# Moving the first attention unit's key tiles a partition in two parts, and letting the gates share a table load

## The chip, the core and the metric

The kernel runs on one core of a Trainium2 chip. The metric is the device time of one execution in microseconds. Five engines work side by side, each through its own instructions in order: TensorE (PE, with its weight loads as PEld), VectorE (DVE), ScalarE (ACT), GpSimd (POOL) and SyncE (SP, which here only issues DMAs). ACT and POOL issue DMAs too, between their other instructions.

## What is computed

A gated sum of two branches over 2048 tokens of 512 channels, in float32:

```python
g = sigmoid((x * gate_w).sum(-1))
a = attention(x) @ wo      # 32 heads of 16; each token sees 8 keys, at distances 0, 2, ... 14
b = (gelu(x @ w_gate) * (x @ w_up)) @ w_down      # 1792 hidden channels
out = g * a + (1 - g) * b
```

The attention takes `logits = q . k * 0.25` for the 8 keys, with the keys before the first token masked, a softmax over the 8, and the weighted sum of the values.

## The kernel before

All matrix products run on PE. Each float32 operand is split into a high part (rounded to the fp32r format by ACT) and a low part (the rest, a subtraction on DVE, or on POOL's queue as an accumulating DMA), and each product is three matmuls. Tokens are dealt by parity (`par`): even tokens first, then odd, since keys at even distances have the same parity. Within a parity, partition `p` holds 8 consecutive tokens as slots `j`, so `NP` is 8.

The program for parity 0 is: `start()`, which projects queries and keys for all 8 slots by a Strassen-like scheme with four banks at a time; then `ffn(0)`, 14 hidden blocks `f` of 128 channels, in whose first two blocks the values are projected (`values(jj)`), with the down projection of earlier blocks between the products of later ones. For parity 1 the projections are the plain ones and `ffn(1)` follows. The out projection comes last.

The attention itself runs on DVE beside all that. It is a Python generator, `attention()`, over 8 units of 128 channels, four for each parity: `load_kq` (keys and queries of the unit into the one buffer `kq`), `scores` (four times a product `prod` of line 298 and a sum over 16 channels on line 301, then the mask), `softmax` (max, subtraction on line 314, Exp on ACT on line 316, sum, reciprocal, times the gate `g`) and `mix` (the weighted values). The function `pull` draws on the generator wherever the products of PE leave time by an estimate, and `paced` ties the long operations to the matmul recorded last, so that DVE cannot run ahead of it. The tile framework then schedules all recorded instructions into one fixed order for each engine, by its own estimate of their times.

The first unit is special. Its keys and queries are not read back from DRAM: `take_first` copies them from PSUM straight into `kq` (`put(0)` to `put(3)` early in `start()`, `put(4)` to `put(7)` at its end; the copies stand in the trace as `kq<-p` and `kq<-acc`). Each partition also needs the 7 key slots before its own 8. These are its neighbour's slots, and `load_kq(0, 0)` moves them a partition down by two DMAs on SP's queue (line 276; 112 and 15 partitions of 7 slots of 512 bytes), after POOL has zeroed the first partition's.

The gates, `1 / (1 + exp(-z))` of the column `z` that `take` collects with the values, are computed in `gates(par)` as soon as the last values of a parity are taken (lines 239 to 243): Exp on ACT, three small operations on DVE. ACT's functions come in table sets. Exp and Gelu are in different sets, so an Exp among the Gelus of `gate_up` costs a table load in front of it and another one in front of the next Gelu.

Other lines that the prediction speaks of: 189 (projections on PE), 211 (copies of the values out of PSUM), 436 (sums of the next blocks' weights, `combine`), 454, 455 and 459 (their operands, `g<-raw`: low part by ACT and POOL's DMA, high part), 497 (gate and up products on PE), 502 (`copy`, a PSUM bank into `s`), 507 (`add`, a bank and `s` into `c`), 511, 513 and 514 (`hidden`), 537 (down projection), 571 (a bank copied into another), 586 and 602 (the two Gelus).

Of the kernel before, what the change touches and what calls it, by code (L numbers as in the profile page):

```python
# [16 lines left out]
P = 128  # L17
# [3 lines left out]
NP = NT // 2  # L21
# [16 lines left out]
BT = 4  # L38
# [9 lines left out]
def tile_gated_mix(ctx: ExitStack, tc: tile.TileContext, xt, wqkv, wff, wo, out):  # L48
    nc = tc.nc
# [17 lines left out]
    def bank(tag):  # L67
        return psum.tile([P, 512], F32, name=tag, bufs=BUFS.get(tag, 1))
# [114 lines left out]
    def qkv_mm(ps, par, jj, cb, kcs, c0=0, cn=512):  # L183
        t = slice((jj % BT) * P, (jj % BT + 1) * P)
        for kc in kcs:
            xh, xl = X[par, jj // BT, kc]
            wh, wl = WC[cb, kc]
            for n, (a, w) in enumerate(((xh, wh), (xl, wh), (xh, wl))):
                LAST[:] = [nc.tensor.matmul(ps[:, :cn], a[:, t], w[:, c0:c0 + cn], start=(kc == 0 and n == 0),  # L189
                                            stop=(kc == KC - 1 and n == 2))]  # L190

    KQ = []

    def take_first(ps, jj, copy):

        if not KQ:
            KQ.append(pool.tile([P, 3 * NP - 1, UC], F32, name="kq"))
        st = tl(next(stages))[:, :CU].rearrange("p (a d) -> p a d", a=2)
        two = ps.rearrange("p (a c d) -> p c a d", a=2, c=2)
        copy(KQ[0][:, NP - 1 + jj::NP], two[:, 0])  # L200
        copy(st, two[:, 1])
        for a, t in enumerate((KS[0, 0][1, W:], QS[0, 0][1])):
            nc.sync.dma_start(t.rearrange("(p j) d -> j p d", j=NP)[jj], st[:, a])
# [4 lines left out]
    def take(ps, par, jj, hh, vals, tag=None):  # L208
        st = tl(tag or next(stages))[:, :512]
        n = CU if vals else 512  # L210
        nc.scalar.activation(st[:, :n], ps[:, :n], AF.Copy)
        two = st.rearrange("p (a c d) -> p a c d", a=2, c=2)
        dst = VS[par, hh] if vals else KS[par, hh]
        queue = nc.sync if (vals if par else not vals) or hh and not vals else nc.scalar
        queue.dma_start(rows(dst[:, W:], jj), two[:, 0])  # L215
        if not vals:
            queue.dma_start(rows(QS[par, hh], jj), two[:, 1])
        elif not hh:
            nc.scalar.activation(z[:, par, jj:jj + 1], ps[:, CU:CU + 1], AF.Copy)

    def project(par, cb, bg=iter(())):
        for jj in range(NP):
            if cb == 1:
                for hh in range(2):

                    ps = bank(f"acc{(2 * jj + hh) % BT}")
                    qkv_mm(ps, par, jj, 1, range(KC), (CU, 0)[hh], (WQ, CU)[hh])
                    take(ps, par, jj, hh, True)
            else:
                ps = bank(next(names))  # L230
                qkv_mm(ps, par, jj, 0, range(KC))
                take(ps, par, jj, 0, False)
            next(bg, None)
            pull((2.7, 2.2)[par])
        done.add((par, cb))
        if cb == 1:
            gates(par)

    def gates(par):
        nc.scalar.activation(en, z[:, par], AF.Exp, scale=-1.0)  # L240
        nc.vector.tensor_scalar_add(en, en, 1.0)
        nc.vector.reciprocal(g[:, par], en)
        nc.vector.tensor_scalar(gc[:, par], g[:, par], -1.0, 1.0, op0=OP.mult, op1=OP.add)

    def values(jj):
        for hh in range(2):
            ps = bank(f"acc{(2 * jj + hh) % BT}")
            qkv_mm(ps, 0, jj, 1, range(KC), (CU, 0)[hh], (WQ, CU)[hh])
            take(ps, 0, jj, hh, True, tag=None if jj < 5 else "c")
        pull(2.7)  # L250
        if jj == NP - 1:
            done.add((0, 1))
            gates(0)

    def project_one(par, jj):

# [10 lines left out]
    def load_kq(par, u):  # L267
        hh, c = divmod(u, 2)
        kq = KQ.pop() if KQ else pool.tile([P, 3 * NP - 1, UC], F32, name="kq")
        k, q = kq[:, :2 * NP - 1], kq[:, 2 * NP - 1:]  # L270
        LG[par, u] = k, q
        if not (par or u):

            nc.gpsimd.memset(k[:1, :NP - 1], 0.0)
            for a, b in (1, P - 15), (P - 15, P):
                nc.sync.dma_start(k[a:b, :NP - 1], k[a - 1:b - 1, NP:])
            return
        load_slots(k, KS[par, hh][c])
        nc.sync.dma_start(q, QS[par, hh][c].rearrange("(p j) d -> p j d", j=NP))

    def load_slots(t, src):
        nc.sync.dma_start(t[:, :NP - 1], src[:S // 2].rearrange("(p j) d -> p j d", j=NP)[:, 1:])
        nc.sync.dma_start(t[:, NP - 1:], src[W:].rearrange("(p j) d -> p j d", j=NP))
# [25 lines left out]
    def softmax(par, u):  # L309
        lg = LG[par, u]  # L310
        m = pool.tile([P, UH, NP], F32, name="m")
        nc.vector.tensor_reduce(m, lg, axis=AX.X, op=OP.max)
        yield 0.7
        nc.vector.tensor_tensor(lg, lg, m[:, :, :, None].to_broadcast([P, UH, NP, W]), op=OP.subtract)
        yield 0.7
        nc.scalar.activation(lg, lg, AF.Exp, scale=DH ** -0.5)
        nc.vector.tensor_reduce(m, lg, axis=AX.X, op=OP.add)
        yield 0.7
        nc.vector.reciprocal(m, m)
        nc.vector.tensor_tensor(m, m, g[:, par, None, :].to_broadcast([P, UH, NP]), op=OP.mult)  # L320
        yield 0.4
        nc.vector.tensor_tensor(lg, lg, m[:, :, :, None].to_broadcast([P, UH, NP, W]), op=OP.mult)
        yield 0.7
# [79 lines left out]
    def pull(budget, key=None):  # L403
        credit[0] += budget
        while credit[0] > 0 and (key is None or key not in done):
            with tc.high_priority(offset=-BEHIND):
                c = next(fill, None)
            if c is None:
                credit[0] = 0.0
                return  # L410
            credit[0] -= c
        if key:
            credit[0] = 0.0
# [78 lines left out]
    def product(ps, a, w, start):  # L492
        for kc in range(2):
            ah, al = XOP[a, kc]
            wh, wl = (x[:, kc * P:(kc + 1) * P] for x in w)
            for n, (w_, a_) in enumerate(((wh, ah), (wh, al), (wl, ah))):
                LAST[:] = [nc.tensor.matmul(ps, w_, a_, start=(start and kc == 0 and n == 0),  # L497
                                            stop=(kc == 1 and n == 2), skip_group_check=True)]

    def copy(ps):  # L500
        s = tl("s")
        nc.scalar.activation(s, ps, AF.Copy)  # L502
        return s

    def add(ps, s):
        c = tl("c")[:, :512]
        nc.vector.tensor_tensor(c, ps, s, op=OP.add)  # L507
        return c
# [44 lines left out]
    def gate_up(par, f, pieces, do):  # L553
# [4 lines left out]
        def idle(i, n):  # L558
            for x in do.get(i, ()):
                x()  # L560
            pull(n * PACE[par] * (1.0 if par or f + 1 < FC else 0.8))

        def piece(i):
            for x in pieces[i]:
                x()
# [7 lines left out]
        piece(0)  # L573
        Z_ = bank("p")
        product(Z_, "s1", w["t1"], True)
        p5 = copy(Z_)
        idle(2, 0.3)
# [9 lines left out]
        idle(5, 0.7)  # L587
        product(Z_, "s4", w["b22"], False)
        c12 = add(Z_, u2)
        idle(6, 0.5)  # L590
# [239 lines left out]
    row, act, mms = Row(nc.vector), Row(nc.scalar), Row(nc.tensor)  # L830
# [5 lines left out]
    def start():  # L836
# [98 lines left out]
        def block(ps, a, w, first, kcs=(0, 1)):  # L935
            for t in range(BT):
                for kc in kcs:
                    ah, al = OP_[a, kc]
                    wh, wl = OP_[w, kc]
                    for n, (a_, w_) in enumerate(((ah, wh), (al, wh), (ah, wl))):  # L940
                        mm(ps[t], t, a_, w_, first and kc == 0 and n == 0, kc == 1 and n == 2)
# [10 lines left out]
        def put(jj, ps):  # L952
            take_first(ps, jj, lambda o, i: act.activation(o, i, AF.Copy))
# [29 lines left out]
            lo("t1", k)  # L983
        put(2, V_[2])
        put(3, V_[3])
        Z_ = [bank("p") for _ in range(BT)]
        block(Z_, "s1", "t1", True)
        p5 = [tl("hh")[:, :512] for _ in range(BT)]
# [66 lines left out]
        def sums(f):  # L1055
            r = RAW[f].rearrange("p (a c) -> p a c", c=QW)
            q_ = {n: r[:, i] for i, n in enumerate(QUARTS)}
            sub(r[:, 0:6:5], r[:, 3::4], r[:, 2:4])
            sub(q_["t2"], q_["b22"], q_["t1"])
            sub(q_["t4"], q_["b21"], q_["t2"])  # L1060
# [23 lines left out]
        parts(1)  # L1084
        put(BT + 2, U[2])
        put(BT + 3, U[3])
        sums(1)
        for n, blk, k in (("a11", 0, 0), ("a12", 0, 2), ("a22", 1, 2)):
            for kc in range(2):
# [66 lines left out]
```

## Time and profile before

| | |
|---|---|
| median of 3 runs | 610.23 us (608.02 to 610.64) |
| the profiled execution | 612.35 us, of which its span (first to last instruction) is 610.6 us |
| mean granted TensorE clock | 0.999 |
| PE busy | 598.4 us (98% of the span), 2802 matmuls recorded |
| DVE busy | 526.0 us (86%) |
| ACT busy | 388.7 us (64%) |
| moved by DMA | 131.03 MB, mean 215 GB/s |

A busy PE in this profile is not PE at its peak, since matmuls overlap and their ends are modelled; what the profile shows reliably of PE is where it is not busy and whom it waits for there. A row of a timeline gives start, duration, engine, line, operation, tiles and count, and in brackets the idle time of the engine just before it and what released it. "SPq" and "ACTq" are DMA issues on those queues.

### The profile page before, as it was taken

What the parts mean: (1) busy time and instruction counts of PE and PEld (TensorE: products, weight loads), DVE (VectorE), ACT (ScalarE), POOL (GpSimd) and SP (SyncE); (2) the same over time, 40 slices, a digit from 0 to 9 for tenths busy, and PEclk for the clock granted to TensorE, in tenths of its full rate; (3) what the DMA queues carried; (4) which work ended last, traced back from release to release, by engine and by line L of the source; (5) the groups of instructions that cost most, each with busy time, mean ns of one, the idle gap of its engine ahead of it and who ended that gap; (6) DMA issues with size and microseconds to landing.
All of it is one profiled execution on the core that took longest, in us unless ns stands there. A gap on an engine that the chain in (4) does not pass through costs nothing.

```text
span 610.6 us, 8186 instructions
## 1 busy us (share of the span) xinstructions
PE 598.4 (98%) x2802; PEld 498.0 (82%) x2802; DVE 526.0 (86%) x611; ACT 388.7 (64%) x653; POOL 79.2 (13%) x106
## 2 busy tenths in 40 slices
PE   8999999899999999999999999999999999999996
PEld 6889977778878788888899887888888888888885
DVE  5992798989998888799988997999799979999882
ACT  5844576678666867777374347556865676684722
POOL 0501001111111111102000001111111111101200
PEclk9999999999999999999999999999999999999999
DMA  7288798699898989876689879686878886938714
GB/s 279 70 250 234 205 285 239 159 290 233 229 248 240 266 234 267 219 226 184 204 224 302 275 241 287 163 236 162 248 168 221 210 261 137 279 108 202 91 38 171
DMA packets 84583, 131.03 MB, mean 215 GB/s; under 512 B 7999, under 2 KB 52159, under 8 KB 84542
## 3 DMA queue, kind: packets, MB, share of 16 engines
q1 hardware_dynamic: 63310, 94.27, 47.8%
q0 software_dynamic: 12096, 31.40, 27.0%
q10 hardware_dynamic: 9136, 4.85, 2.6%
q8 instruction: 22, 0.36, 0.2%
q14 instruction: 19, 0.16, 0.1%
HBM read 67.18 MB, written 36.77 MB: 170 GB/s over the span
## 4 chain that ended last, share of the span: by engine, by line
PE 79%; DMA 8%; issue 7%; ACT 2%; DVE 1%; SPq 1%; ACTq 1%; POOL 0%; POOLq 0%; DVEq 0%
PE p L497 35%; PE acc L537 11%; PE p L537 11%; PE acc L189 9%; PE p L763 5%; DMA g<-raw 4%; PE p L828 3%; PE acc L828 2%; PE p L189 2%; PE acc L763 2%; DMA raw<-wff 1%; DMA prod<-wqkv 1%; DMA ws<-g 1%; ACTq L215 1%; DMA vs<-c 1%
## 5 line engine op out<-in xcount | busy, mean ns | idle before, releaser
L497 PE MATMUL p<-S,g 128*128 128x512 f32 x672 | 165.7, 389 | 1.0 <-ACT s L502 1.0
L497 PEld LDWEIGHTS p<-S,g 128*128 128x128 f32 x672 | 125.8, 188 | 27.4 <-ACT s L502 1.4
L497 PE MATMUL p<-A,g 128*128 128x512 f32 x504 | 128.2, 391 | 4.4 <-DMA g<-raw 2.4
L497 PEld LDWEIGHTS p<-A,g 128*128 128x128 f32 x504 | 93.8, 188 | 26.3 <-DMA g<-raw 4.3
L298 DVE TENSOR_TENSOR prod<-kq 128x2048 f32<-128x2048 f32 x32 | 73.1, 2284 | 20.5 <-DMA kq<-kq 14.1
L336 DVE TENSOR_TENSOR prod<-v,lg 128x2048 f32<-128x2048 f32 x32 | 73.0, 2281 | 4.2 <-PE p L497 2.0
L455 POOL DMA_DIRECT2D g<-raw x40 | 34.5, 863 | 316.2 <-ACT g L454 162.3
L301 DVE TENSOR_REDUCE lg<-prod 128x128 f32<-128x2048 f32 x32 | 73.0, 2282 | 0.3
L537 PE MATMUL p<-d,hh 128*128 128x512 f32 x224 | 68.1, 390 | 0.0
L537 PE MATMUL acc<-d,hh 128*128 128x512 f32 x224 | 61.3, 390 | 0.2 <-DMA d<-r 0.2
L502 ACT ACTIVATE s<-p 128x512 f32<-128x512 f32 x56 | 33.3, 595 | 28.7 <-PE p L497 23.6
L537 PEld LDWEIGHTS acc<-d,hh 128*128 128x128 f32 x224 | 41.9, 188 | 9.7 <-DMA d<-r 1.1
L537 PEld LDWEIGHTS p<-d,hh 128*128 128x128 f32 x224 | 42.0, 188 | 8.9 <-ACT hh L513 0.3
L459 ACT ACTIVATE g<-raw 128x1024 fp32r<-128x1024 f32 (+1 forms) x40 | 39.4, 989 | 10.3 <-PE p L497 10.1
L507 DVE TENSOR_TENSOR c<-p,s 128x512 f32<-128x512 f32 x56 | 38.0, 682 | 8.1 <-PE p L497 7.8
L514 DVE TENSOR_TENSOR hl<-c,hh 128x512 fp32r<-128x512 f32 x56 | 38.3, 683 | 7.2 <-ACT hh L513 6.5
L511 DVE TENSOR_TENSOR c<-c 128x512 f32<-128x512 f32 x56 | 38.3, 683 | 6.2 <-ACT c L602 5.9
L537 PE MATMUL p<-d,hl 128*128 128x512 f32 x112 | 42.6, 389 | 0.0
L454 ACT ACTIVATE g<-raw 128x1024 fp32r<-128x1024 f32 (+1 forms) x40 | 39.4, 985 | 4.6 <-DVE raw L436 3.0
L513 ACT ACTIVATE hh<-c 128x512 fp32r<-128x512 f32 x56 | 35.0, 626 | 10.2 <-DVE c L511 10.0
L340 DVE TENSOR_TENSOR prod<-prod 128x1024 f32<-128x1024 f32 x32 | 39.0, 1220 | 0.4
L550 ACT ACTIVATE rt<-p 128x512 f32<-128x512 f32 x48 | 28.2, 593 | 17.4 <-PE p L537 16.9
(194 smaller groups left out, 918.6 us busy)
## 6 DMA issues: line engine op xcount, KB each, us to landing
g<-raw POOLq DMA_DIRECT2D x27, 512.0 KB, 6.8
raw<-wff SPq DMA_DIRECT2D x42, 256.0 KB, 3.7
ws<-g SPq DMA_DIRECT2D x14, 768.0 KB, 6.3
g<-ws SPq DMA_DIRECT2D x14, 768.0 KB, 5.9
r<-wff SPq DMA_DIRECT2D x28, 256.0 KB, 4.1
d<-r POOLq DMA_DIRECT2D x26, 256.0 KB, 6.4
g<-raw POOLq DMA_DIRECT2D x13, 384.0 KB, 7.3
v<-vs SPq DMA_DIRECT2D x8, 512.0 KB, 6.8
```

The lines of the kernel that those rows point to most:

```text
L189: LAST[:] = [nc.tensor.matmul(ps[:, :cn], a[:, t], w[:, c0:c0 + cn], start=(kc == 0 and n == 0), stop=(kc == KC - 1 and n == 2))]
L298: paced(nc.vector.tensor_tensor(prod, spans(k, jj), q[:, jj:jj + 2, None, :].to_broadcast([P, 2, W, UC]), op=OP.mult))
L301: nc.vector.tensor_reduce(two_of(lg, jj), prod.rearrange("p j w (h d) -> p (j w) h d", d=DH), axis=AX.X, op=OP.add)
L336: paced(nc.vector.tensor_tensor(prod.rearrange("p j w (h d) -> p (j w) h d", d=DH), spans(v, jj).rearrange("p j w (h d) -> p j w h d", d=D ...
L340: nc.vector.tensor_tensor(prod[:, :, :4], prod[:, :, :4], prod[:, :, 4:], op=OP.add)
L454: nc.scalar.activation(lo, raw, AF.Copy, scale=-1.0)
L459: ins = nc.scalar.activation(hi, raw, AF.Copy)
L497: LAST[:] = [nc.tensor.matmul(ps, w_, a_, start=(start and kc == 0 and n == 0), stop=(kc == 1 and n == 2), skip_group_check=True)]
L511: nc.vector.tensor_tensor(ge, ge, up, op=OP.mult)
L514: nc.vector.tensor_tensor(hl_, ge, hh_.bitcast(F32), op=OP.subtract)
L537: LAST[:] = [nc.tensor.matmul(pp, a[:, ts], w, start=(i == 0 and n == 0 and gr == 0), stop=(i == 1 and n == 2), skip_group_check=True)]
L763: LAST[:] = [nc.tensor.matmul(pa, a, b, start=(first and n == 0), stop=(last and n == 2), skip_group_check=True)]
```

## The change

`load_kq(0, 0)` no longer issues the two DMAs. `start()` does it through a new helper `shift`: slots 0 to 2 (whose sources `put(1)` to `put(3)` write) by two DMAs on SP's queue right behind `put(3)`, slots 3 to 6 by two DMAs on ACT's queue behind `put(7)`. There `act` is the wrapper that keeps ACT's instructions of `start()` in the order written. The zeroing by POOL moves along with it. And `gates(par)` is no longer called at the end of the values, but from `softmax` of the first unit of each parity, behind its Exp.

```diff
@@ project
         done.add((par, cb))
-        if cb == 1:
-            gates(par)
@@ values
         if jj == NP - 1:
             done.add((0, 1))
-            gates(0)
@@ load_kq
         if not (par or u):
-
-            nc.gpsimd.memset(k[:1, :NP - 1], 0.0)
-            for a, b in (1, P - 15), (P - 15, P):
-                nc.sync.dma_start(k[a:b, :NP - 1], k[a - 1:b - 1, NP:])
             return
@@ softmax
         nc.scalar.activation(lg, lg, AF.Exp, scale=DH ** -0.5)
+        if not u:
+            gates(par)
         nc.vector.tensor_reduce(m, lg, axis=AX.X, op=OP.add)
@@ start
         put(2, V_[2])
         put(3, V_[3])
+        k0 = KQ[0][:, :2 * NP - 1]
+        nc.gpsimd.memset(k0[:1, :NP - 1], 0.0)
+
+        def shift(queue, i, j):
+            for a, b in (1, P - 15), (P - 15, P):
+                queue.dma_start(k0[a:b, i:j], k0[a - 1:b - 1, NP + i:NP + j])
+
+        shift(nc.sync, 0, BT - 1)
...
         put(BT + 2, U[2])
         put(BT + 3, U[3])
+        shift(act, BT - 1, NP - 1)
         sums(1)
```

In the built program the instructions of the engines stand in a partly different order from the first hidden blocks on, since the framework schedules anew. On ACT the two DMA issues stand between the bank copy of line 571 and the first copy of line 502. ACT's table loads fall from 21 to 19.

## The prediction

> **What bounds the kernel now.** I read the page's head first, then the busy time of each engine by stretches of 20 us, then the list of PE's own waits.
>
> ```profile
> span 610.6 us, 8186 instructions
> ```
>
> ```profile
> 40.00:60.00 20.00, 19.99 (x131) 17.95 (x130) 9.76 (x16) 9.24 (x22) 1.79 (x2) 1.00 0.84 231
> ...
> 100.00:120.00 20.00, 17.99 (x78) 14.16 (x77) 20.00 (x22) 13.84 (x23) 2.89 (x4) 1.00 0.59 143
> ...
> 240.00:260.00 20.00, 20.00 (x90) 16.57 (x89) 15.40 (x15) 14.54 (x25) 2.90 (x4) 1.00 0.89 223
> ```
>
> ```profile
> PE p L497 <- DMA g<-raw: 2.4, 3, 1.3
> PE p L497 <- DVE c L507: 2.0, 1, 2.0
> PE p L78 <- DVE zero L72: 1.1, 1, 1.1
> PE p L497 <- ACT s L502: 1.0, 1, 1.0
> ```
>
> The stretches give PE, PEld, DVE, ACT and POOL in that order, then clock, DMA share and GB/s. PE is busy 19.99 of 20 us while the values begin and 20.00 of 20 in the row from 240, so there it sets the pace and nothing that other engines win can show. It falls back in a few places, and the waits name them: 2.4 us for operands that POOL's DMAs complete, 2.0 us for one add on DVE, 1.0 us for one copy on ACT (the 1.1 us are at the start). That is 5.4 us that work on DVE, ACT and the queues could win at most by these rows, 0.9% of the span. The stretch from 100 shows which engine was short: DVE is busy all of its 20.00 us there, PE 17.99.
>
> So the question is whether DVE's and ACT's work around those three places comes earlier or later, and only that.
>
> **Part 1: the shift.** Here are the copy after which ACT is to issue, the shift as it is now, and DVE's first score; then two waits of other engines, and how long the shift's DMAs took to land.
>
> ```profile
> 48.30 0.65 ACT L571 ACTIVATE p<-p 128x512 f32<-128x512 f32 x1
> ...
> 57.49 2.88 SPq L276 DMA_DIRECT2D kq<-kq  x2
> ...
> 64.44 2.29 DVE L298 TENSOR_TENSOR prod<-kq 128x2048 f32<-128x2048 f32 x1 [14.08 <-DMA kq<-kq]
> ```
>
> ```profile
> ACT hh L211 <- DMA qs<-hh: 4.8, 1, 4.8
> ```
>
> ```profile
> SPq L430 <- DVE raw L828: 5.2, 2, 5.0
> ```
>
> ```profile
> DMA to landing us min/median/max: 4.9/5.8/6.7
> ```
>
> The last slots are copied before the bank copy that ends at 48.95. SP gets to the shift at 57.49 only, because other issues stand ahead of it, and DVE sits idle for 14.08 us until 64.44. In the built order of the changed program ACT issues the second part right behind the copy that ends at 48.95. With the first landing at its maximum, 6.7 us, the tiles are there at 48.95 + 6.7 = 55.65; the second DMA, issued half of 2.88 us later and landing in 4.9, comes at 55.3. I take 55.7, which is 8.7 us ahead of now. The bounds: each DMA carries 4 of 7 slots, so a smaller one may land in the 4.9 us (53.9); if the second takes the longest issue and landing together, 48.95 + 2.88 + 6.7 = 58.5.
>
> What ACT pays: two issues, 2.88 us on SP's queue as measured, perhaps less where a queue is quiet. Behind them wait the copy of line 502, the operand casts of line 454 with POOL's DMAs behind these, and the copies of the values. I cost them at nothing, because ACT sits idle for 4.8 us a little later, waiting for the DMA that frees a staging buffer. Without that cover they would cost up to 2.9 us.
>
> The first part goes to SP's queue in front of the loads of line 430, which wait 5.0 us for DVE in that place. It is hidden there, and SP's later issues at 57.49 lose the 2.88 us in front of them. The zeroing on POOL is free at both places.
>
> The moved bytes are the same. But four slots, 127 x 4 x 512 bytes = 0.26 MB, now run between 49 and 56 us, and at the 231 GB/s of the row from 40 this is 1.1 us of all engines' work, in front of the stores for which ACT waits. [...]
>
> **Part 2: the gates.** ACT now, around the gates, with PE's wait behind them:
>
> ```profile
> 79.26 1.28 ACT L240 ACT_TABLE_LOAD   x1 [0.37 <-ACT z L219]
> 80.55 0.21 ACT L240 ACTIVATE en<-z 128x8 f32<-128x8 f32 x1
> ...
> 83.09 1.28 ACT L602 ACT_TABLE_LOAD   x1
> 84.38 0.60 ACT L602 ACTIVATE c<-p 128x512 f32<-128x512 f32 x1
> 84.87 0.59 ACT L502 ACTIVATE s<-p 128x512 f32<-128x512 f32 x1
> ```
>
> ```profile
> 85.52 0.73 PE L497 MATMUL p<-S,g 128*128 128x512 f32 x2 [1.02 <-ACT s L502]
> ```
>
> A load, the small Exp, a load back for Gelu, and only then the copy for which PE stands 1.02 us. In the changed order this pair of loads stays where it is, and the unit's own Exp joins it, directly behind the small one and ahead of everything else. What goes is the unit's own pair of loads, 2 x 1.28 = 2.56 us of ACT some 15 us later, where PE waits for no copy of ACT. So the saving buys nothing, and the Exp moves in front of a copy that PE does wait for.
>
> ```profile
> L298 DVE TENSOR_TENSOR prod<-kq 128x2048 f32<-128x2048 f32 x32 | 73.1, 2284 | 20.5 <-DMA kq<-kq 14.1 <-PE p L497 3.7 <-DMA kq<-qs 1.5
> L301 DVE TENSOR_REDUCE lg<-prod 128x128 f32<-128x2048 f32 x32 | 73.0, 2282 | 0.3
> ...
> L507 DVE TENSOR_TENSOR c<-p,s 128x512 f32<-128x512 f32 x56 | 38.0, 682 | 8.1 <-PE p L497 7.8
> ...
> L436 DVE TENSOR_TENSOR raw<-raw 128x256 f32<-128x256 f32 x24 | 10.0, 418 | 0.1
> ...
> L316 ACT ACTIVATE lg<-lg 128x512 f32<-128x512 f32 x8 | 5.1, 632 | 0.1
> ```
>
> When can that Exp start? It needs the subtraction of line 314. In the changed order of DVE there stand, from the first score to that point, eight long operations and nine short ones: 8 x 2.28 = 18.2 us, and between 9 x 0.42 = 3.8 and 9 x 0.68 = 6.1 for the short ones, 22.0 to 24.3; I take 23.5, nearer to the 0.68 because most of the nine are whole 512-wide adds. From 55.7 that is 79.2. But DVE's first gate operation stands just ahead of the subtraction and waits for the small Exp, which ends at 80.76. So the subtraction ends at about 81.6 (0.16 us, an estimate for the tiny one, and 0.68), and ACT, ready at 80.76, stands 0.84 us and then takes 0.63 us for the Exp. The chain behind it, up to the copy at 84.87, is 1.4 us later, and so is PE: its 1.02 us grow to 2.4. The bounds are 0 (if the copy is not the last thing PE waits for there) and the case of the rival below.
>
> **Part 3: what the lead buys.** The second of the three places, and how the DVE backlog ends:
>
> ```profile
> 107.85 0.68 DVE L507 TENSOR_TENSOR c<-p,s 128x512 f32<-128x512 f32 x1
> ...
> 108.58 0.73 PE L497 MATMUL p<-A,g 128*128 128x512 f32 x2 [2.01 <-DVE c L507]
> ...
> 124.23 0.96 PE L497 MATMUL p<-A,g 128*128 128x512 f32 x3 [1.30 <-DMA g<-raw]
> ...
> 134.91 0.69 DVE L317 TENSOR_REDUCE m<-lg 128x64 f32<-128x512 f32 x1 [3.02 <-ACT lg L316]
> ```
>
> PE stands 2.01 us until the add that begins at 107.85. From 64.44 to 134.91 DVE works off a backlog, and idles for 3.02 us only at its end. An 8.7 us lead reaches into that. In the changed order one long operation more stands ahead of this add (2.28 us, the scheduler spends part of the lead on scores); the wait for the small Exp takes 1.6 us (79.2 to 80.8), and I estimate 1.5 us of new waiting for the second unit's keys: their load waits on the first unit's scores and 1.5 us of idle stand in front of that unit now (the L298 row). Left are 8.7 - 2.28 - 1.6 - 1.5 = 3.3 us: the add begins near 104.5, before PE gets there. This wait goes, 2.0 us.
>
> The waits for POOL's operand DMAs (2.4 us in three places; the one shown ends at 124.23) hang on DVE's sums of line 436 ahead of ACT and POOL. By the same count these are at most a microsecond earlier, and PE arrives 0.6 us earlier, so I leave them as they are. Behind 134.91 DVE is no longer late, and PE's row from 240 has no idle time; whatever is won or lost by then is carried to the end unchanged.
>
> **Sum.** +1.4 (the copy behind the Exp) - 2.0 (the add) + 0 (shift issues) + 0 (operand DMAs) = -0.6 us. The profiled execution took 612.35 us, 1.75 us around its span of 610.6; it would be 611.75. The median of the runs shown is 610.23, 2.1 us below the profiled execution, so I forecast 609.6 us.
>
> **The rivals.**
>
> *The lead cures more.* If DVE's lead reaches ACT and POOL as well, the operand waits vanish with the add's and the copy stays at its 1.02 us: 2.4 + 2.0 = 4.4 us, 610.2 - 4.4 = 605.8 us. For it: DVE's 20.00 of 20 us just where PE falls back, and 14.08 us of idle right before. Against it: the changed order gives the lead to scores first, and one of the operand waits lies beyond 134.91, where DVE is not late any more.
>
> *The Exp stands in ACT's way for longer.* ACT takes its instructions in order, and the unit's Exp stands ahead of the copies. It decides from the point at which DVE is not done with the first unit when the small Exp is: first score later than 80.76 - 23.5 = 57.3. With the upper bound of 58.5 and the short operations at their upper 6.1, the subtraction ends at 58.5 + 24.3 + 0.16 = 83.0 where 81.6 was counted, another 1.4 us; the two issues' 2.88 us uncovered at the same time would not add, since they lie earlier. If in addition the lead is then too small for the add, nothing is taken off, and a third of the operand waits, 0.8 us, comes once more: 610.2 + 1.4 + 1.4 + 0.8 = 613.8 us. For it: a landing of 6.7 us is no exception in these queues, and the changed order was made from estimates of such landings. Against it: 58.5 needs the longest issue and the longest landing at once.
>
> *The crowded DMA engines.* The 1.1 us of part 1 reach PE through ACT's wait for the staging buffer: 609.6 + 1.1 = 610.7 us. Against it: PE's list has no wait for those copies.
>
> *Nothing moves.* If DVE's lead is only turned into idle time and ACT's saving lies off the path, as in the row from 240: 610.2 us.
>
> **How the numbers follow.** About 0.5%, 3.05 us, is what a measurement of this kernel can tell from no change; its three runs lie 2.6 us apart. The forecast has 0.36, crowding 0.12, nothing 0.10: all within 0.5%, 0.58 together. The larger cure, 0.72% below, has 0.22; the longer stand of ACT, 0.59% above, 0.20. The range runs from the one to the other, 605.8 to 613.8, with a tenth of the chance beyond each end.
>
> **What would show it.** In the profile of the changed kernel: DVE's first score at 54 to 58.5 with 4 to 8 us of idle before it; one table load for the small Exp and the unit's Exp near 80, and ACT's idle time before the latter (0.84 us by my count); PE's wait for the copy of line 502 near 86 us at about 2.4; no wait for the add of line 507 near 107; the operand waits at some 2.4 in sum. The forecast is wrong if PE's waits for ACT, DVE and DMA sum to less than 2.4 us or more than 8.5 us, or if PE gets idle time behind 240 us, where it has none now.

## The result, and the profile after

| | before | after |
|---|---|---|
| median (lowest to highest), 20 executions each | 615.67 us (608.02 to 618.12) | 608.28 us (606.52 to 611.49) |
| the profiled execution, its span | 612.35, 610.6 us | 609.62, 607.8 us |
| ACT busy | 388.7 us | 386.1 us |

The ratio of after to before is 0.9934, with a 95% interval of 0.9906 to 0.9962: faster by 0.66%, with the whole interval below 1. The kernel before has two groups of times. In the experiments below it was executed 117 times: 62 with a mean granted clock of 0.996 or more took 611.03 us in the mean, 55 with 0.995 or less took 617.89 us. The order of the changed kernel was executed 44 times (above, in e2 and in e11), never below 0.996, with a mean of 608.6 us. (In the profiles the clock is also at half for up to 2.9 us at the end of the span, which lowers this mean by up to 0.002, and one stretch of 3.4 us lowers it by 0.003. Nine of the 44 have 0.996 or 0.997, which leaves room for one such stretch.) So there are two gains: 2.4 us between the executions with 0.996 or more, and a low clock that came in 55 of 117 executions before and in none of 44 after. (The ratio leaves out the longest executions, so it shows only a part of the second.)

PE's own waits in the profile after, with total, number and longest (line numbers are now smaller by 6: 491 was 497, 496 was 502, 501 was 507, 531 was 537):

```profile
PE p L491 <- ACT s L496: 2.0, 1, 2.0
PE acc L531 <- DMA d<-r: 1.4, 1, 1.4
PE p L78 <- DVE zero L72: 1.1, 1, 1.1
PE acc L822 <- DVE A L822: 0.7, 1, 0.7
PE p L491 <- DMA g<-raw: 0.6, 1, 0.6
```

The wait for the add is gone, the operands' fell from 2.4 to 0.6, the copy's rose from 1.0 to 2.0, and a wait for the down weights is new (0.2 before). From 5.6 us the four kinds come to 4.0. Busy time by stretches, in the prediction's columns, first of the kernel before, then of the changed one:

```profile
40.00:240.00 200.00, 194.48 (x937) 161.58 (x936) 171.07 (x203) 138.31 (x229) 28.96 (x34) 1.00 0.88 241
240.00:590.00 350.00, 349.85 (x1634) 293.31 (x1633) 315.65 (x348) 220.39 (x367) 40.59 (x51) 1.00 0.76 207
```

```profile
40.00:240.00 200.00, 195.98 (x951) 164.50 (x950) 174.78 (x204) 137.15 (x231) 29.34 (x34) 1.00 0.88 244
240.00:590.00 350.00, 350.00 (x1635) 293.37 (x1634) 317.19 (x351) 218.97 (x363) 40.05 (x50) 1.00 0.76 205
```

By 240 us PE has begun 14 matmuls more, at 350.00 / 1635 = 0.214 us each 3.0 us of work; the busy time shows only 1.5 of it, since ends are modelled. Behind 240 PE is full in both. The shift and the first score, from the timeline after:

```profile
48.37 0.63 ACTq L822 DMA_DIRECT2D kq<-kq  x1
49.04 1.37 ACTq L822 DMA_DIRECT2D kq<-kq  x1
50.45 0.60 ACT L496 ACTIVATE s<-p 128x512 f32<-128x512 f32 x1 [1.35 <-PE acc L189]
...
52.99 2.29 DVE L290 TENSOR_TENSOR prod<-kq 128x2048 f32<-128x2048 f32 x1 [2.48 <-DMA kq<-kq]
```

DVE starts 11.45 us earlier than before (64.44). ACT pays 2.0 us for the two issues and is idle for PE right behind them. Then the rows around the gates, with PE's wait behind them, and around the add:

```profile
77.84 0.39 ACT L211 ACTIVATE c<-acc 128x256 f32<-128x256 f32 x1 [4.11 <-DMA vs<-c]
...
80.83 0.21 ACT L237 ACTIVATE en<-z 128x8 f32<-128x8 f32 x1
81.87 0.63 ACT L308 ACTIVATE lg<-lg 128x512 f32<-128x512 f32 x1 [0.83 <-DVE lg L306]
...
86.01 0.59 ACT L496 ACTIVATE s<-p 128x512 f32<-128x512 f32 x1
...
86.66 1.66 PE L491 MATMUL p<-S,g 128*128 128x512 f32 x6 [1.97 <-ACT s L496]
```

```profile
102.36 1.28 DVE L501 TENSOR_TENSOR c<-p,s 128x512 f32<-128x512 f32 x2
104.22 0.63 ACT L477 ACTIVATE d<-r 128x512 fp32r<-128x512 f32 x1 [1.99 <-PE acc L531]
```

The Exp stands where the prediction put it, behind 0.83 us of idle time. The add comes at 102.36, where PE no longer waits for it.

### The profile page after: what moved, and what is told of

It reads as the page before. It is cut to its first block, busy times and chain, and to the rows that moved or that the text cites. A ratio compares the mean times of both kernels' runs of the same rounds, so it can differ in the third digit from the quotient of the medians.

```text
span 607.8 us, 8199 instructions
## 1 busy us (share of the span) xinstructions
PE 596.7 (98%) x2802; PEld 498.0 (82%) x2802; DVE 528.3 (87%) x611; ACT 386.1 (64%) x651; POOL 79.1 (13%) x106
## 4 chain that ended last, share of the span: by engine, by line
PE 85%; issue 9%; DMA 4%; ACT 1%; POOL 0%; SPq 0%; DVE 0%; POOLq 0%; ACTq 0%; DVEq 0%
PE p L491 38%; PE p L531 12%; PE acc L531 11%; PE acc L189 10%; PE p L757 5%; PE acc L822 3%; PE p L822 3%; PE p L189 2%; PE acc L757 2%; DMA raw<-wff 1%; DMA g<-raw 1%; DMA prod<-wqkv 1%; POOL g L449 0%; ACT g L448 0%; SPq L845 0%
## 5 line engine op out<-in xcount | busy, mean ns | idle before, releaser
L491 PE MATMUL p<-A,g 128*128 128x512 f32 x504 | 126.7, 390 | 0.6 <-DMA g<-raw 0.6
L531 PE MATMUL acc<-d,hh 128*128 128x512 f32 x224 | 58.7, 390 | 1.4 <-DMA d<-r 1.4
```

Of the source, the lines that this page charges most:

```text
L531: LAST[:] = [nc.tensor.matmul(pp, a[:, ts], w, start=(i == 0 and n == 0 and gr == 0), stop=(i == 1 and n == 2), skip_group_check=True)]
```

## The experiments

Each was timed 12 times, beside 35 executions of the kernel before per chip: median 611.94 us with e1 to e4, 612.86 with e5 to e8, 616.71 with e9 to e12.

**e1: the kernel before, unchanged.**

> The kernel before, unchanged, profiled once more. The theory of the DVE lead: first score near 64, an add of DVE for which PE waits some 2 us near 107, sum of PE's idle time between 80 and 220 us near 5.5 us when the run takes about 610 us. Its times lie in two groups, near 610 and near 616. If the group near 616 shows up in this profile, the theory that these too come from late operands expects some 6 us more idle time of PE between 80 and 240 us; the rival, that a shared resource outside the order is slower (transfers or the clock), expects longer transfers or slower matmuls spread over the whole span.

614.44 us (609.93 to 619.74), ratio 1.0008 (0.9962 to 1.0055). Its profiled execution fell in the upper group: 618.12 us, clock 0.990. Its stretches, cut near where the clock record changes, and two rows of its timeline:

```profile
100.00:109.00 9.00, 6.92 (x29) 4.80 (x28) 9.00 (x11) 6.30 (x11) 0.85 (x1) 1.00 0.51 121
109.00:112.50 3.50, 3.50 (x11) 2.68 (x10) 3.50 (x5) 1.14 (x3) 0.00 (x0) 0.52 0.72 247
112.50:126.00 13.50, 11.56 (x51) 9.22 (x49) 12.40 (x12) 7.91 (x12) 2.58 (x3) 1.00 0.70 179
126.00:133.00 7.00, 5.28 (x12) 4.13 (x13) 2.57 (x4) 1.13 (x2) 0.00 (x0) 0.52 0.94 276
```

```profile
108.08 2.04 PE L497 MATMUL p<-A,g 128*128 128x512 f32 x6 [2.02 <-DVE c L507]
...
127.72 4.63 PE L497 MATMUL p<-A,g 128*128 128x512 f32 x10 [3.67 <-DMA g<-raw]
```

The clock was granted at 0.5 for 3.4 us (from 109.1) and for 6.8 us (from 126.2), behind or within PE's waits for the add and for operands: just the waits that the change removes or shortens. PE worked in 8.7 of these 10.2 us (from 126.2 to 127.7 it stood), so the half clock cost it some 4.4 us, half of the 8.7: an estimate, after the 2.93 us that six matmuls take at 0.5 in e9, where others take 1.52 at 1.0. Its waits for ACT, DVE and DMA come to 7.7 us, where the first profile of the same order has 5.4. The theory that the upper group comes from late operands expected some 6 us more, and it is 2.3; the rival expected slower matmuls over the whole span, and they stand in two short stretches. That waits can cause a fall of the clock is tested by e7 to e9.

**e2: the changed kernel with the gates called in their old place.**

```diff
+        if cb == 1:            # project; likewise gates(0) in values
+            gates(par)
...
-        if not u:              # softmax
-            gates(par)
```

> The change without the gates' move: shift in two parts as in the changed kernel, gates called where they were. In the built program every engine's order is the same as in the changed kernel, table loads included (19). Theory (all of the gain is the shift): the changed kernel's time, 608.3 us or a ratio to before within 0.003 of the changed kernel's 0.9934. Rival (the gates' move shares in it): at least 1 us slower than the changed kernel, 609.3 or more.

608.00 us (606.34 to 611.83), ratio 0.9945 (0.9909 to 0.9981), the time of the changed kernel. The built programs say why: apart from line numbers, all five engines have the same order with the gates in either place, and the kernel before with only the gates moved has exactly the order of the kernel before (e1 stands for it). This half of the change does nothing. The shared table load comes from the shift: e3, which leaves the gates where they were, has 19 loads too.

**e3: the kernel before with the old, undivided shift, still issued from `load_kq`, on ACT's queue instead of SP's.**

```diff
-                nc.sync.dma_start(k[a:b, :NP - 1], k[a - 1:b - 1, NP:])
+                nc.scalar.dma_start(k[a:b, :NP - 1], k[a - 1:b - 1, NP:])
```

> The kernel before, with one edit: the two DMAs of the shift, whole, in their old place in the program, are issued by ACT instead of SP. The scheduler puts them between ACT's copies right behind the last key copy. Theory (what counts is when DVE's first score can start): first score at 53 to 56, the changed kernel's gain within 1 us, 607.5 to 609.3. Rival (the two parts matter, since seven slots crowd the DMA engines where four did not): 1 to 2 us slower than the changed kernel.

607.90 us (607.08 to 608.91), ratio 0.9910 (0.9875 to 0.9945). DVE's first score starts at 55.0 us.

```profile
PE p L497 <- ACT s L502: 1.5, 1, 1.5
PE p L497 <- DMA g<-raw: 1.3, 2, 0.8
```

One word gives the whole gain. Neither the division in two parts nor the place in `start()` is needed. But the word changes more than the queue: the framework schedules all engines anew, and on DVE at least 85 of the 611 instructions have another place among the others than before. No run keeps the old order and moves the shift alone, so what the early start is worth by itself, and what the new order, stays open.

**e4: the changed kernel with the shift undivided, behind `put(7)`, on SP's queue.**

```diff
-        shift(nc.sync, 0, BT - 1)
...
-        shift(act, BT - 1, NP - 1)
+        shift(nc.sync, 0, NP - 1)
```

> The change with the shift undivided and on SP's queue, written behind the last key copy. In the built order it stands ahead of the next weights' loads there. Theory (start of the first score): SP is free for it at about 54 us, landing 5 to 7 us later, first score near 60, half of the lead; time between before and after, 608.5 to 610. Rival (ACT's issue itself is what helps, or costs): as before, 610, or better than the changed kernel.

614.09 us (612.31 to 616.36), ratio 1.0023 (0.9990 to 1.0057). On SP the shift is issued at 53.9 and the first score starts at 62.3, a lead of 2.2 us. The theory's 608.5 to 610 us was missed; its time is that of the kernel before.

```profile
PE p L491 <- ACT s L496: 3.5, 2, 2.7
PE acc L189 <- ACT z L219: 2.0, 2, 1.8
PE p L491 <- DMA g<-raw: 1.9, 2, 1.5
```

So the place in `start()` alone gains nothing. The lead of 2.2 us comes with none of the gain, the 9.4 us of e3 with all of it. That the lead is the reason is not shown by this run: the wait for the add is gone here as well, and what costs are two waits for ACT, 3.5 us for the copy and 2.0 us for `z`, in an order of its own. Here, too, the clock was at 0.5, from 89.5 to 96.3, around the wait of 2.7 us.

**e5 and e12: the changed kernel with the first unit's Exp tied to the matmul recorded last.**

```diff
-        nc.scalar.activation(lg, lg, AF.Exp, scale=DH ** -0.5)
+        ex = nc.scalar.activation(lg, lg, AF.Exp, scale=DH ** -0.5)
+        if not (par or u):
+            paced(ex)
```

> The changed kernel, with the first unit's Exp tied to the matmul recorded last, so that it stands some 25 ACT instructions later, behind the copies, with a pair of table loads of its own (21 loads instead of 19). If PE's wait of 1.97 us near 86 us is the Exp standing in front of the copy on ACT (0.83 us idle and 0.63 us of work), it falls by 1.46 us to about 0.5 us and the time goes from 608.3 to about 606.8 us. Rival: the pair of loads that comes back (2 x 1.28 us) is met by another copy or operand that PE waits for, and the time stays at 608 to 610 us. In either case no fall of the granted clock, since no wait of PE grows beyond 2 us.

> The changed kernel with the first unit's Exp behind the copies, on the same chip as the changed kernel itself: 606.9 us, 1.3 us faster than the changed kernel, if the wait for the copy is a cost of its own; the same time as the changed kernel, if the earlier difference was between chips or runs.

e5: 606.95 us (605.57 to 609.42), ratio 0.9925 (0.9896 to 0.9954). e12, on the chip on which the changed kernel took 608.34: 607.03 us (604.96 to 613.24), ratio 0.9921 (0.9885 to 0.9957). It is the fastest version by its median, twice, by 1.3 us; the intervals of its ratios and those of the changed kernel overlap, so the step beyond the changed kernel is not settled. The time was as expected, the reason was not. Waits of e5:

```profile
PE p L493 <- ACT s L498: 1.1, 1, 1.1
...
PE p L493 <- DMA g<-raw: 0.4, 1, 0.4
```

The wait for the copy did not fall to 0.5; it is 1.1 us here and 1.6 in e12, with ACT standing 2.1 and 2.6 us for a store (`vs<-c`) ahead of that copy. What both profiles lack is the wait for the down weights, 1.2 to 1.7 us in those of the changed order: in the new order of ACT their cast starts at 101.2, where it started at 104.22. Two of the 24 executions, both in e12, had a clock of 0.995 or less.

**e11: the changed kernel again.**

> The changed kernel once more, to be read against the other runs on the same chip: 608.3 us, waits of PE of 2.0 us (copy) and 1.4 us (down weights) or less.

608.34 us (607.16 to 612.98), ratio 0.9930 (0.9894 to 0.9966). With e2 this is a third profile of the same order, and it says what the wait for the copy varies with. ACT's and PE's waits in e11, and two rows of ACT's timeline:

```profile
ACT c L211 <- DMA vs<-c: 1.2, 1, 1.2
...
PE p L491 <- ACT s L496: 1.0, 1, 1.0
```

```profile
79.18 0.63 ACT L308 ACTIVATE lg<-lg 128x512 f32<-128x512 f32 x1 [0.83 <-DVE lg L306]
...
81.46 0.38 ACT L211 ACTIVATE c<-acc 128x256 f32<-128x256 f32 x1 [1.16 <-DMA vs<-c]
```

In the changed kernel's first profile ACT stood 4.11 us for the landing of the values' stores (`vs<-c`) and PE 2.0 us for the copy; here 1.2 and 1.0; in e2 ACT 0.2 and PE none. The Exp had 0.83 us of idle and 0.63 us of work in front of the copy in all three. So what differs from one to the next is the landing of the stores, not the Exp. In e11 ACT stands for a store behind the Exp once more (81.46), so there the Exp is not what the copy waits for. In the first profile the late store lies ahead of the gates' table load, and the Exp's 1.46 us do stand between it and the copy; how much of the 2.0 us is the Exp's was not told apart.

**e6: the changed kernel with the gates as 0.5 + 0.5 tanh(z/2).**

```diff
-        nc.scalar.activation(en, z[:, par], AF.Exp, scale=-1.0)
-        nc.vector.tensor_scalar_add(en, en, 1.0)
-        nc.vector.reciprocal(g[:, par], en)
-        nc.vector.tensor_scalar(gc[:, par], g[:, par], -1.0, 1.0, op0=OP.mult, op1=OP.add)
+        nc.scalar.activation(en, z[:, par], AF.Tanh, scale=0.5)
+        nc.vector.tensor_scalar(g[:, par], en, 0.5, 0.5, op0=OP.mult, op1=OP.add)
+        nc.vector.tensor_scalar(gc[:, par], en, -0.5, 0.5, op0=OP.mult, op1=OP.add)
```

> The changed kernel with the gates computed as 0.5 + 0.5 tanh(z/2): Tanh is in Gelu's table set, so the gates need no load and no reciprocal (17 loads instead of 19). DVE, which stands 3.37 us for the small Exp near 81 us, would get it 1.28 us earlier, the unit's Exp would follow its own load, and the copy behind it would come about 1.3 us earlier: PE's wait near 86 us 0.7 instead of 1.97 us, 607.0 us. Rival: what DVE does before PE's next waits (0.6 us for operands, 1.4 us for the down weights) is not the limit and the chain on ACT is as long, since the load for the Exp now stands behind the small Tanh: wait of 2 us as before, 608.3 us.

608.53 us (607.14 to 611.43), ratio 0.9942 (0.9907 to 0.9977): the rival's number, with 17 table loads as expected. None stands in front of the Tanh at 76.83; the 1.28 us load at 77.06, for the unit's Exp, follows it.

```profile
82.28 0.39 ACT L211 ACTIVATE c<-acc 128x256 f32<-128x256 f32 x1 [2.81 <-DMA vs<-c]
...
86.06 2.48 PE L490 MATMUL p<-S,g 128*128 128x512 f32 x6 [1.84 <-ACT s L495]
```

The Exp is done at 79.0, but ACT then waits 2.81 us for a store, and PE for the copy as before. Six matmuls took 2.48 us, where the same row of the changed kernel (86.66) has 1.66: the clock was at 0.5 for 3.4 us from 86.6, behind this wait of 1.84. The expectation had a wait of 2 us for its rival, but no fall of the clock; e5's expected none up to 2 us, and this one stands behind 1.84.

**e7, e8, e9: one wait put in where PE had none.** The changed kernel with a chain of 6, 10 or 14 copies of a bank onto itself on ACT, in block 6 of the second parity; PE's order is the same in all three.

```diff
+        if par and f == 6:
+            for _ in range(6):          # 10 in e8, 14 in e9
+                HOLD[:] = [nc.scalar.activation(X_, X_, AF.Copy)]
+                paced(HOLD[0])
         product(X_, "s3", w["t3"], False)   # this and the next matmuls come after HOLD
```

> The changed kernel with a chain of 6 copies of a PSUM bank onto itself on ACT (about 0.6 us each) in front of one product of block 6 of the second parity, and PE's next matmuls held behind it: one wait of PE put in, in a place (near 430 us) where it had none. By the theory that PE's clock falls to half for 3.4 or 6.8 us after waits of some 2 us and more, this run costs its wait, 0.5 to 2.5 us, and in some of its executions 1.7 or 3.4 us more, with a mean granted clock of 0.995 or less. By the rival, that the low clocks of the kernel before come from the chip and not from waits of PE, all executions stay in one group with a clock of 0.997 or more.

> As with six copies, but ten, so that PE's wait is about 2.5 us longer, with the same order on PE. By the theory of the clock: the time above that of six copies is 2.5 us for the wait and, in most executions, 1.7 to 3.4 us more, with clock records at 0.5 for 3.4 or 6.8 us right behind the wait. By the rival: 2.5 us more and nothing else, one group, no record at 0.5 between start and end.

> As with ten copies, but fourteen: the longest of PE's inserted waits, the one behind the chain near 444 us, grows from 1.71 us by four copies of 0.61 us to about 4.1 us, with the same order on PE. Against ten copies (612.6 us) that alone is 615.0 us: this is what the rival expects (the low clocks come from the chip, not from waits of PE), with no record at 0.5 in the middle of the span. By the theory of the clock, a wait of 4.1 us is beyond those of 2.0 to 2.9 us behind which falls were recorded, so that nearly all executions have the clock at 0.5 for at least 3.4 us right behind 444 us and a time of 616.7 us (one stretch of 3.4 us) to 618.5 us (6.8 us), at mean granted clocks of 0.994 to 0.997.

610.99, 612.60 and 617.76 us (ratios 1.0001, 0.9971 to 1.0031; 1.0009, 0.9974 to 1.0044; and 1.0065, 1.0025 to 1.0106). Six copies did not make the wait that was meant, behind the chain, but two others of 1.0 and 1.3 us, and the time is 2.7 us above the changed kernel's 608.28; eleven executions have a clock of 0.997 or more, one has 0.995, so e7 decides nothing. In e8 the wait behind the chain is 1.54 us, and the time 1.6 us more than in e7:

```profile
446.21 1.66 PE L491 MATMUL p<-S,g 128*128 128x512 f32 x6 [1.54 <-ACT p L593]
```

Its profile has the full clock until the end of the span; eleven of its 12 executions have a clock of 0.999 or 1.000, and one has 0.997 (615.10 us), which leaves room for one short stretch. My expectation of falls in most of e8's executions was wrong; its wait stayed under 2 us. Four copies more, in e9:

```profile
122.34 1.20 PE L491 MATMUL p<-A,g 128*128 128x512 f32 x4 [2.52 <-DMA g<-raw]
...
444.81 1.52 PE L491 MATMUL p<-A,g 128*128 128x512 f32 x6
450.35 2.93 PE L491 MATMUL p<-S,g 128*128 128x512 f32 x6 [4.01 <-ACT p L593]
...
458.57 1.52 PE L491 MATMUL p<-A,g 128*128 128x512 f32 x6
```

```profile
449.00:456.00 7.00, 5.65 (x13) 4.46 (x14) 4.30 (x5) 1.99 (x5) 0.00 (x0) 0.52 0.29 74
```

Six matmuls of one shape take 1.52 us ahead of the wait, 2.93 behind it and 1.52 again later (1.66 behind the shorter wait of e8); the record has the clock at 0.5 from 449.2 for 6.8 us. All 12 executions have clocks of 0.992 to 0.997, 0.995 in the mean where e8 has 0.999. The added wait is 2.47 us and the time 5.16 us more than in e8. The clock's share of that is at most the 2.7 us left: e9 ran on another chip than e8, and its profile has 2.7 us of waits for operands where e8's has 0.6. By the mean clocks it is about 2.5 us (0.004 of 616). The rival (the chip lowers the clock by itself) expected 615.0 and no record at 0.5 in the middle of the span. PE's order is the same in e8 and e9, and the fall stands at the one wait that was made longer: a wait of PE can cause it. It need not: the wait of 2.52 us for operands, in the same profile (122.34), passed at full clock. And the expectation's "2.0 to 2.9 us" was not what the records show; until then falls had come behind waits of 1.84 to 3.67 us.

**e10: the changed kernel with the first score's product and sum computed three times.**

```diff
-        for jj in range(0, NP, 2):
+        for jj in ((0, 0, 0) if not (par or u) else (0,)) + (2, 4, 6):
```

> The changed kernel with the first score's product and sum computed three times over, which is 4 DVE operations of 2.28 us, 9.1 us, directly behind the earlier key tiles: the shift's place and queue stay, DVE's lead of 11.4 us is eaten but for 2.3 us. If the gain comes through DVE's lead, PE's wait of 2 us for the add near 107 us and the longer waits for operands (2.4 to 5.2 us) are back, falls of the clock in part of the executions too, and the median is that of the kernel before, 611 to 613 us. Rival: the gain comes from the queues (SP's later loads no longer stand behind the shift, the Exp shares a load), not from DVE: 608 to 609 us, no such waits.

618.94 us (618.02 to 622.33), ratio 1.0101 (1.0063 to 1.0138). Both theories missed:

```profile
PE p L757 <- ACT hh L86: 8.4, 1, 8.4
PE p L491 <- ACT p L565: 2.8, 2, 2.5
```

No wait came back near 107 us. By the code, the extra steps also draw on the planner's account (`pull`), which puts the attention's later work off: DVE's last transpose came at 600.72 instead of 590.80, and the out projection waited 8.4 us for what follows from it. So this run does not test the lead. A version with the extra work outside the planner's account was not run, and with e4's waits for ACT no run here varies the lead alone.

## Why the prediction was right, and where not

**What bounds the kernel.** Right: what changed are the waits of the three places, with a new one of 1.4 us for the down weights near 109, and PE's row behind 240 stayed full.

**The shift.** The first score was forecast for 55.7 (53.9 to 58.5) and came at 52.99, outside the bounds, with 2.48 us of idle before it where 4 to 8 were given. The step that failed is the landing: I took 4.9 to 6.7 us from the row of landings, and the second DMA, of 15 partitions, was there 52.99 - 49.04 = 3.95 us after its issue at the latest. The issues cost 2.0 us on ACT, and PE has no wait there, as said; but the cover was another one, 1.35 us of ACT's idle time for PE right behind the issues. What the other issuer changed is the place in the queue: in e3 the same DMAs, from ACT's queue, began 9.2 us earlier (48.27 for 57.49).

**The gates.** The "pair of loads stays and the unit's Exp joins it" was right as an order, and its cause was wrong: moving the shift does it, the edit of the gates nothing (e2, e3). The rival that the change doesn't do what it says should have been put for this half alone.

**The copy, +1.4.** The Exp's part was forecast well, 0.83 us of idle time against 0.84, and in one profile the wait was 2.0 for 2.4. But the term lacked the stores: with the same Exp in the same place the wait was 2.0, 1.0 and none, as the values' stores landed. I had set ACT's waits for its DMAs aside, "against it: PE's list has no wait for those copies"; they reach PE through ACT's order, where the copy of line 502 stands behind the stores' copies. That the shift's own DMAs crowd these stores, as that rival had it, is not shown: all three profiles have the same DMAs.

**The add, -2.0.** Right: gone in all three profiles. The add began at 102.36 for 104.5, from a lead 2.7 us larger than forecast; DVE's wait for the small Exp took 3.4 us of it for 1.6, and the 1.5 us of new waiting for the second unit's keys did not come in the first profile.

**The operands, 0.** They fell, from 2.4 to 0.6, 0.8 and 1.7 us, as the rival of the larger cure had it, and the wait for the down weights took their place with 1.4, 1.2 and 1.7 us. Together 2.6 us (5.2 in e1) became 2.0, 2.0 and 3.4: as a sum, not clearly changed.

**The sum.** -0.6 us were forecast. The waits of the list fell by 1.6, and the executions with a clock of 0.996 or more by 2.4 us. By 608.28 us the forecast of 609.6 is 1.3 us too high; by the ratio the change lies beyond 0.5%, on the side to which I gave 0.22. That the number came so near is in part luck. The copy's term varied by 2 us from profile to profile, and the base of 610.23 left out the group with the low clock: between the medians of 20 the change is 7.4 us, of which 0.6 were forecast.

**What is missing.** No step and no rival had the clock. I priced a wait of PE at its own length, and took the base from three executions whose times (608.02 to 610.64) all lie in the group of the full clock; of 117, 55 lay in the other. Those took some 7 us more, 617.89 against 611.03. In the one profile of such an execution (e1) the falls stand at the add's wait and at one for operands. So the waits on the list were dearer than their rows; how much of the 7 us hangs on the add's alone was not told apart.

## What to carry to other kernels

Ask of a late DMA first on which queue it stands: here one word (SP to ACT) brought DVE's start forward by 9.4 us and gave the whole gain, and the elaborate part of the change added nothing that the times show. Read several profiles of the same order before a wait is given a cause, since here it went from 2.0 to 0 with the landing of stores. And count a wait of the matrix engine dearer than its length where it is as long as those at which the clock fell here: seven of 1.84 to 8.4 us. Before a time of three executions is taken as the base, look whether the kernel has a second group of times.

## What the runs showed of the hardware

PE's granted clock has two values in the records of all 14 profiles, 1.0 and 0.5, and stretches at 0.5 in mid-span last 3.4 or 6.8 us. They stood behind or at the end of waits of 1.84 (e6), 2.02 and 3.67 (e1), 2.5 and 8.4 (e10, mean clock 0.990), 2.7 (e4) and 4.01 us (e9). Waits of 1.97 us (the changed kernel), 2.01 us (the kernel before, in the first profile) and 2.52 us (e9, for operands) passed without one, and in e8, with 1.54 us as its longest, the profile shows none. So between 1.84 and 2.52 us some waits had a fall and others none, and no run shows what decides it; every longer wait in the lists of these profiles (2.7, 3.67, 4.01 and 8.4 us) had a fall. Six matmuls of 128x512 that took 1.52 us at 1.0 took 2.93 us at 0.5 (e9).
